# Starting every transferred SBUF buffer at a multiple of 512 bytes in a fused attention and feed-forward kernel

## The chip, the cores and the metric

The kernel runs on one core of a Trainium2 chip. The metric is the device time of one execution in microseconds (us), of which several runs are taken; the median counts.

## The reference

Two stages follow each other. The first is attention with a local window, a few global keys and a bias that falls linearly with distance; the second is a gated feed-forward layer on its output.

```
scores = q k^T / sqrt(64)                       # 4 batches, 8 heads, 768 rows, 64 columns
keep   = (key < 8) or (0 <= row - key < 96)
scores = where(keep, scores - 2^-(head+1) * distance, -1e9)
x      = softmax(scores) v                      # 3072 rows of 512
h      = x w_in                                 # 512 x 2048
out    = (h * sigmoid(1.702 h)) w_out           # 2048 x 512
```

q, k and v are float32. The two weights arrive as float64 and are converted on the chip.

## The kernel before

The 3072 rows are 24 blocks of 128. A block's keys are its own 128 and the last of the block before, with the 8 global keys copied over a few columns of these. The first four blocks (one for each batch) have no block before them, and are computed by another path. Numbers are carried as pairs of float16, a high and a low part, and a product is three matmuls (high times high, high times low, low times high).

For a later block, `prep` (L561) loads q, k and v into `raw` (L443), splits q and k into float16 pairs in `qk` (L510 on ScalarE, L511 on VectorE), turns them by a transposing DMA into `QK` (L513), and makes a second copy of the turned keys with its two halves swapped by two plain DMAs (L515). `halves` (L518) splits v into `VR`. For each pair of heads, `unit` (L574) computes scores on TensorE (L591), adds the mask and takes the minimum on VectorE (L597, into `NM`), exponentiates on ScalarE (L607, the sums of exponentials into `sm`), splits the probabilities `p` into `hl` (L611, L612), turns `hl` by a transposing DMA into `pt` (L613), and multiplies by the values on TensorE (L622 to L624). `finish` (L719) divides by the sums (L739 to L741), splits into `x16` (L763, L765) and turns that into `xT` (L766). `handover` (L546) does the same preparation for the keys and values of a batch's first block: its buffers carry `over` in their names. It also keeps the 8 global keys in `KG` (L527, copied into each block's keys at L538) and the global values in `VG` (L533, copied at L715).

The weights are loaded into `ws` (L238), converted on VectorE and ScalarE (L412 to L418) and kept in SBUF as float16 pairs. The feed-forward layer takes two blocks at a time: `up` (L853) and, for later pairs, `up_two` (L893, with sums at L898 to L909) compute h, L862 to L865 and L925 to L934 the gated product `g`, and `pile` (L961) the sum over 2048 rows of the second weight, written out from `yo` (L977, L994). Late in the run inputs and weights are loaded once more for range checks (`again`).

The order of the instructions is made by a planner (`Work.order`, L136) from estimated costs, due times and a table of offsets (`NUDGE`, L30); every engine then runs its fixed list, and waits by semaphores where data isn't there. SP's queue issues nearly all DMAs, in the planner's order.

A buffer of the planner is a `Buf` in a `Ring` of a few slots (L83 to L105). When a `Buf` is first used, it takes a tile from a pool by its tag, or, where its ring has fixed tiles (`r_hl`), a view of one of these. Two pools lie one behind the other in SBUF: `const`, with what lives through the run, and `sb`, with the rings. A tile's size is rounded up to 32 bytes per partition, and the next begins there, so that one tile of odd size moves the beginnings of all behind it.

Of the kernel before, what the change touches and what calls it, by code (L numbers as in the profile page):

```python
# [8 lines left out]
F32 = mybir.dt.float32  # L9
# [10 lines left out]
P = 128  # L20
# [62 lines left out]
class Ring:  # L83


    def __init__(self, pool, tag, bufs, loose=False, psum=False):
        self.pool, self.tag, self.bufs, self.loose, self.line, self.psum = pool, tag, bufs, loose, [], psum
        self.tiles = None


class Buf:
# [8 lines left out]
    def __call__(self):  # L100
        if self.ring.tiles:
            return self.view(self.ring.tiles[self.i % self.ring.bufs])
        if self.t is None:
            self.t = self.ring.pool.tile(self.shape, self.dtype, tag=self.ring.tag, name=self.name, bufs=self.ring.bufs)
        return self.t  # L105


# [12 lines left out]
class Work:  # L120
# [5 lines left out]
    def add(self, on, fn, after=(), bufs=(), want=1e9):  # L126
        t = Task(on, fn, [a for a in after if a is not None], bufs, want)
        t.tag = self.tag + ("l" if "SP" in on else "")
        for a in t.after:
            a.next.append(t)  # L130
        for b in t.bufs:
            b.users.append(t)
        self.tasks.append(t)
        return t
# [107 lines left out]
def kernel(  # L242
# [12 lines left out]
    B, H, S, D = q.shape  # L255
# [11 lines left out]
    const = ctx.enter_context(tc.tile_pool(name="const", bufs=1))  # L267
# [30 lines left out]
    swt = const.tile([P, 2, NST], F32, name="swt")  # L298
    e2 = const.tile([P, 2, 4 * NST], F32, name="e2")
    junk = const.tile([P, 1024], BF16, name="junk")  # L300
    back = const.tile([P, 1], F32, name="back")
    nc.vector.memset(back, 0.5 / (SG * SW))


    def ring(tag, bufs, pool=sb, loose=False):
        return Ring(pool, tag, bufs, loose, pool is not sb)

    r_raw, r_qk16, r_QK, r_KG = ring("raw", 2), ring("qk16", 1), ring("QK", 3), ring("KG", 1)
    r_VR, r_VG, r_sm = ring("VR", 4), ring("VG", 1), ring("sm", 3)
    r_pr, r_hl, r_pt = ring("pr", 2), ring("hl", 2), ring("pt", 4)  # L310
    r_hl.tiles = [const.tile([P, 8 * P], F16, name=f"hl{j}") for j in range(2)]
    r_VF = ring("VF", 3, loose=True)
    r_x, r_x16, r_xT, r_xS = ring("x", 1), ring("x16", 1), ring("xT", 2), ring("xS", 2)
    r_ws, r_wa = ring("ws", 3), ring("wa", 2, loose=True)
# [80 lines left out]


    WT, W_ready, squared, checks = {}, {}, {}, []

    def weights(s, u):

        nm = f"{s}_{u}"
        ws = Buf(r_ws, [P, 1024, 2], I32, "ws" + nm)
        wa = Buf(r_wa, [P, 1024], F32, "wa" + nm)
        w = WT[s, u] = Buf(r_w[s, u], [P, 2, 1024], F16, "w" + nm)
        ai = lambda: wa().bitcast(I32)
        extra = lambda: w().bitcast(I32).rearrange("p z c -> p (z c)")
        low = lambda: w().bitcast(U16).rearrange("p z (c t) -> p (z c) t", t=2)[:, :, 0]
        t0 = add({"SP": 2.75}, lambda e: load_weights(nc, ws(), w_in, w_out, s, u), bufs=[ws])

        t3 = add({"DVE": 0.61}, lambda e: nc.vector.tensor_scalar(  # L412
            extra(), ws()[:, :, 1], -2 ** 31, -2 ** 30, ALU.bitwise_and, ALU.bitwise_xor), [t0], [ws, w])
        t4 = add({"ACT": 1.21}, lambda e: nc.scalar.mul(low(), ws()[:, :, 0].bitcast(U32), LAST * 2.0 ** -29), [t3], [ws, w])
        t5 = add({"DVE": 1.15}, lambda e: nc.vector.scalar_tensor_tensor(
            ai(), ws()[:, :, 1], 3, extra(), ALU.logical_shift_left, ALU.bitwise_xor), [t3, t4], [ws, w, wa])
        t6 = add({"ACT": 0.96}, lambda e: nc.scalar.mul(w()[:, 0], wa(), SW), [t5], [wa, w])
        t7 = add({"DVE": 1.15}, lambda e: nc.vector.scalar_tensor_tensor(  # L418
            w()[:, 1], wa(), SW, w()[:, 0], ALU.mult, ALU.subtract), [t6], [wa, w])
        W_ready[s, u] = t7  # L420
        early_ = s % 2 and u == 0
        checks.append(add({"ACT": 1.05}, lambda e: nc.scalar.activation(
            junk, w()[:, 0], AF.Square, accum_out=swt[:, u, s:s + 1]), [t7], [w], 140.0 if early_ else 270.0 + 18.0 * (2 * s + u)))
        squared[s, u] = checks[-1]
        if not early_:
            checks[-1].soon = 200.0 + 18.0 * (2 * s + u)
# [8 lines left out]
    blk, prev = {}, {}  # L435

    def place(n):

        return (n, 0) if n < EARLY else ((n - EARLY) // (NB - 1), 1 + (n - EARLY) % (NB - 1))

    def load(n, raw, parts=(0, 1, 2)):
        b, i = place(n)
        return [add({"SP": 1.2 if n < 2 and 2 not in parts else 1.35}, lambda e, z=z: nc.sync.dma_start(  # L443
            raw()[:, z], (q, k, v)[z][b, :, i * P:(i + 1) * P, :].rearrange("h p d -> p h d")), bufs=[raw]) for z in parts]
# [9 lines left out]
    def prep_first(n):  # L454

        raw = Buf(r_raw, [P, 3, H, D], F32, f"raw{n}")
        QZ = Buf(r_w[NST - 1 - n // 2, n % 2], [P, 2, NU, P], F32, f"QZ{n}")
        KF = Buf(r_hl, [P, NU, P], F32, f"KF{n}", lambda t: t.bitcast(F32).rearrange("p (u t) -> p u t", u=NU))
        d = blk[n] = dict(QZ=QZ, KF=KF, sm=Buf(r_sm, [P, 2 * H], F32, f"sm{n}"))

        def clean(e):
            for z in range(2):
                part = slice(D * z, D * z + D)
                if e == "ACT":
                    nc.scalar.mul(QZ()[part, 1 - z], idle[part].rearrange("p (u t) -> p u t", u=NU), 0.0)
                else:
                    nc.gpsimd.memset(QZ()[part, 1 - z], 0.0)

        zero = add({"ACT": 1.2} if n < 2 else {"POOL": 1.2}, clean, bufs=[QZ], want=-10.0 if n < 2 else 1e9)
        ld = load(n, raw, (0, 1))  # L470
        turned = []
        for z in range(2):
            tq = Buf(r_y[1, z] if n == 0 else r_h, [P, NU, P], F32, f"tq{n}_{z}")

            def turn(e, z=z, tq=tq):
                for u in range(NU):
                    nc.tensor.transpose(tq()[:, u], raw()[:, z, 2 * u:2 * u + 2, :].rearrange("p h d -> p (h d)"), ident)

            turned.append((tq, add({"PE": 4 * TURN}, turn, ld[z:z + 1], [raw, tq])))

        def taken(to, z, part):
            tq, t1 = turned[z]
            return add({"ACT": 0.6, "DVE": 0.7}, lambda e: (
                nc.scalar.mul(to(), tq()[part], SX) if e == "ACT" else nc.vector.tensor_scalar(to(), tq()[part], SX, None, ALU.mult)),
                [t1], [tq, KF if z else QZ])

        rows = [slice(D * z, D * z + D) for z in range(2)]
        d["qk_ready"] = [zero, *(taken(lambda z=z: QZ()[rows[z], z], 0, rows[z]) for z in range(2)), taken(KF, 1, slice(0, P))]
# [10 lines left out]
    def turn_halves(n, raw, QK, ld, a0):  # L499

        qk = Buf(r_qk16, [P, 2, H, 2, D], F16, f"qk16{n}_{a0}")

        def rq():
            return raw()[:, a0:2].rearrange("p a h d -> p (a h) d")

        def part(z):
            return qk()[:, a0:, :, z].rearrange("p a h d -> p (a h) d")

        f = 1.0 if a0 == 0 else 0.55
        t1 = add({"ACT": f * 0.96}, lambda e: nc.scalar.mul(part(0), rq(), SX), ld, [raw, qk])  # L510
        t2 = add({"DVE": f * 1.15}, lambda e: nc.vector.scalar_tensor_tensor(part(1), rq(), SX, part(0), ALU.mult, ALU.subtract),  # L511
                 [t1], [raw, qk])
        t3 = add({"SP": f * 2.8}, lambda e: nc.sync.dma_start_transpose(  # L513
            QK()[:, a0:2].rearrange("p a h t -> p (a h) t"), qk()[:, a0:].rearrange("p a h z d -> p (a h z d)")), [t2], [qk, QK])
        return [add({"SP": 0.4}, lambda e, z=z: nc.sync.dma_start(  # L515
            QK()[64 * z:64 * z + 64, 2], QK()[64 - 64 * z:128 - 64 * z, 1]), [t3], [QK]) for z in range(2)]
# [44 lines left out]
    def prep(n):  # L561

        b, i = place(n)
        raw = Buf(r_raw, [P, 3, H, D], F32, f"raw{n}")
        QK = Buf(r_QK, [P, 3, H, P], F16, f"QK{n}")
        d = blk[n] = dict(QK=QK, sm=Buf(r_sm, [P, 2 * H], F32, f"sm{n}"))
        ld = load(n, raw, (0, 1, 2) if n >= EARLY else (0, 1))
        d["qk_ready"] = turn_halves(n, raw, QK, ld[0:2], 0)
        if n >= EARLY:
            VR = d["VR"] = Buf(r_VR, [P, 2, H, D], F16, f"VR{n}")  # L570
            d["v_ready"] = halves(VR, raw, ld[2:])
            guard(n, raw, ld, start[n // 2, 0] - 40.0 + 20.0 * (n % 2))
# [783 lines left out]
```

## Time and profile before

Three runs took 591.45, 592.07 and 594.02 us, a median of 592.07.

| | us |
|---|---|
| profiled execution | 592.54 |
| its span | 590.6 |
| TensorE (PE) busy | 579.0 |
| VectorE (DVE) busy | 497.1 |
| ScalarE (ACT) busy | 462.6 |
| GpSimd (POOL) busy | 3.7 |

In the profile's rows a group of instructions is named by its line, engine, operation and tiles, output first; "<-" names what ended the engine's idle time before it. PEld is the loading of TensorE's weights, which overlaps the matmuls. SPq is SP's queue, where an instruction's length is the time that its issue took. A DMA share of 1 means that the core's 16 DMA engines had packets under way all the time. SP's queue moved 108.30 MB in 268,032 packets, which took 91.2% of the 16 engines' time. The granted clock of TensorE was 1.00 in nearly all stages.

### The profile page before, as it was taken

The page shows a single profiled execution, that of the slowest core. Times are in us where ns is not written, and L with a number is a line of the kernel's source. Part 1 is how long each engine was busy: PE and PEld are TensorE (multiplying, and loading weights), DVE is VectorE, ACT ScalarE, POOL GpSimd, SP SyncE. Part 2 cuts the span into 40 slices and gives each one's busy share as a digit, 9 for nine tenths or more (in the row PEclk, how much of TensorE's full clock was granted, in tenths as well). Part 3 has the DMA queues.
Part 4 walks back from the last instruction along what each step waited for, and adds up shares of the span by engine and source line. Part 5 has one row for each costly group of instructions (what it writes and reads, how often), then busy time and mean ns, then how long its engine had stood idle before and what let it go on. Part 6 is the DMA issues. An engine that isn't in the chain of part 4 may idle for free. (4 is left out here: it accounts for less than half of the span.)

```text
span 590.6 us, 16904 instructions
## 1 busy us (share of the span) xinstructions
PE 579.0 (98%) x6744; PEld 435.4 (74%) x6744; DVE 497.1 (84%) x1180; ACT 462.6 (78%) x1086; POOL 3.7 (1%) x14
## 2 busy tenths in 40 slices
PE   8999899999999999999999999999999999999997
PEld 5886666777678777877778767787777866875896
DVE  6898899999999999888899799889889878676452
ACT  6678799898768979878798798788987878774351
POOL 2000000000000000000000000000000000000000
PEclk9999999999999999999999999999999999999999
DMA  9998999999968877999999999999999999971101
GB/s 256 294 288 204 283 235 239 201 191 164 189 118 170 147 134 145 201 182 202 228 173 203 203 215 206 192 220 205 241 200 169 224 182 228 216 176 19 37 2 41
DMA packets 268265, 109.57 MB, mean 186 GB/s; under 512 B 249300, under 2 KB 249812, under 8 KB 268180
## 3 DMA queue, kind: packets, MB, share of 16 engines
q1 hardware_dynamic: 268032, 108.30, 91.2%
q8 instruction: 54, 0.88, 0.7%
q14 instruction: 31, 0.25, 0.1%
q10 hardware_dynamic: 148, 0.13, 0.1%
HBM read 57.67 MB, written 6.29 MB: 108 GB/s over the span
## 5 line engine op out<-in xcount | busy, mean ns | idle before, releaser
L961 PE MATMUL y<-w,g 128*128 128x512 f16 (+1 forms) x1248 | 265.1, 363 | 1.6 <-DVE g L865 0.8
L961 PEld LDWEIGHTS <-g 128*128 128x128 f16 x1248 | 118.0, 98 | 108.0 <-DVE g L865 1.8
L893 PEld LDWEIGHTS <-w 128*128 128x128 f16 x1728 | 101.4, 98 | 3.9
L607 ACT ACTIVATE p<-p,NM 128x232 f32<-128x232 f32 x160 | 76.4, 479 | 9.4 <-DVE NM L597 9.1
L893 PEld LDWEIGHTS <-T 128*128 128x128 f16 x1296 | 76.8, 98 | 5.7 <-issue 0.4
L853 PE MATMUL h<-xT,w 128*128 128x256 f16 x576 | 67.1, 273 | 0.2 <-DVE t L863 0.2
L597 DVE CUSTOM_DVE_ANT_0 p<-s,mm 128x232 f32<-128x232 f32 x160 | 57.7, 396 | 9.9 <-PE s L591 9.5
L853 PEld LDWEIGHTS <-w 128*128 128x128 f16 x576 | 55.5, 98 | 7.9 <-issue 0.3
L934 DVE SCALAR_TENSOR_TENSOR g<-t,g 128x512 f16<-128x512 f32 x72 | 49.2, 688 | 10.8 <-ACT g L933 10.5
L612 DVE TENSOR_TENSOR hl<-p,hl 128x464 f16<-128x464 f32 x80 | 51.0, 638 | 5.8 <-ACT hl L611 5.6
L933 ACT ACTIVATE g<-t 128x512 f16<-128x512 f32 x72 | 44.9, 628 | 11.7 <-PE y L961 7.8
L925 ACT ACTIVATE t<-h 128x512 f32<-128x512 f32 (+1 forms) x72 | 35.8, 517 | 18.6 <-DVE h L901 15.8
L611 ACT CAST hl<-p 128x464 f16<-128x464 f32 x80 | 46.0, 575 | 1.8 <-DMA pt<-hl 0.3
L893 PE MATMUL pa<-xS,T 128*128 128x128 f16 x648 | 44.8, 219 | 0.0
L901 DVE TENSOR_TENSOR h<-pb,h 128x256 f32<-128x256 f32 x72 | 28.6, 420 | 18.5 <-PE pb L893 17.1
L591 PEld LDWEIGHTS <-QK 128*128 128x128 f16 x640 | 36.5, 98 | 7.1 <-DVE NM L597 1.7
L926 DVE SCALAR_TENSOR_TENSOR t<-t,h 128x512 f32<-128x512 f32 (+1 forms) x72 | 38.5, 553 | 3.3 <-ACT t L925 3.2
L591 PE MATMUL s<-QK 128*128 128x128 f16 x320 | 38.2, 219 | 0.0
L893 PE MATMUL pa<-xT,w 128*128 128x128 f16 x540 | 37.5, 219 | 0.0
L893 PE MATMUL pb<-xS,w 128*128 128x128 f16 x540 | 37.5, 219 | 0.0
L622 PE MATMUL pv<-VR,pt 128*128 128x64 f16 x288 | 34.5, 193 | 0.8 <-DMA VR<-VG 0.5
L624 PE MATMUL pv<-VR,pt 128*128 128x64 f16 x288 | 34.5, 193 | 0.0
(186 smaller groups left out, 1033.7 us busy)
## 6 DMA issues: line engine op xcount, KB each, us to landing
ws<-in_moe_w_in_dram SPq DMA_DIRECT2D x8, 1024.0 KB
ws<-in_moe_w_out_dram SPq DMA_DIRECT2D x8, 1024.0 KB, 6.6
raw<-in_q_dram SPq DMA_DIRECT2D x24, 256.0 KB, 4.5
raw<-in_k_dram SPq DMA_DIRECT2D x24, 256.0 KB, 5.0
QK<-QK SPq DMA_DIRECT2D x40, 128.0 KB, 5.4
raw<-in_v_dram SPq DMA_DIRECT2D x20, 256.0 KB, 3.5
out_dram<-yo SPq DMA_DIRECT2D x20, 256.0 KB
ws_00again<-in_moe_w_in_dram SPq DMA_DIRECT2D x8, 512.0 KB, 4.1
```

What stands on the lines that cost most here:

```text
L591: nc.tensor.matmul(sp()[:, j, lo:hi], d["QK"]()[:, 0, h, :], K[:, 1 + z, h, P - (hi - lo):], start=(z == 0), stop=(z == 1), skip_group_che ...
L597: nc.vector.tensor_tensor_reduce(out=pr()[:, j, :], in0=sp()[:, j, :], in1=m, scale=-1.0 / SC, scalar=3.0e38, op0=ALU.add, op1=ALU.min, ac ...
L607: ex.append(add({"ACT": 0.473}, lambda e, j=j: nc.scalar.activation(pr()[:, j, :], pr()[:, j, :], AF.Exp, bias=NM[:, n, hs[j]:hs[j] + 1], ...
L611: t4 = add({"ACT": 0.5}, lambda e: nc.scalar.copy(hl()[:, 0, :, SKIP:], pr()), ex, [pr, hl])
L612: t5 = add({"DVE": 0.55}, lambda e: nc.vector.tensor_sub(hl()[:, 1, :, SKIP:], pr(), hl()[:, 0, :, SKIP:]), [t4], [pr, hl])
L853: nc.tensor.matmul(ph()[:, fi, :], w1(s, cc, z, fi), X[:, y, cc, :], start=(j + cc == 0), stop=(j == 2 and cc == NCC - 1))
L893: nc.tensor.matmul(o()[:, fi], w, x()[:, y * NCC + 2 * k + cc, t], start=(first and fi + j + cc == 0), stop=(last and j + cc == 3), skip_g ...
L925: t1 = add({"ACT": 0.06 + 0.22 * w}, lambda e: nc.scalar.activation(o(), src(), AF.Tanh, scale=0.851 / (SX * SW)), after, srcs)
L926: return add({"DVE": 0.08 + 0.265 * w}, lambda e: nc.vector.scalar_tensor_tensor(o(), o(), 1.0, src(), ALU.add, ALU.mult), [t1], srcs)
L933: t4 = add({"ACT": 0.53}, lambda e, g=g, tt=tt: nc.scalar.mul(g()[:, 0], tt(), SG / (SX * SW)), u, [tt, g])
L934: t5 = add({"DVE": 0.61}, lambda e, g=g, tt=tt: nc.vector.scalar_tensor_tensor(g()[:, 1], tt(), SG / (SX * SW), g()[:, 0], ALU.mult, ALU.s ...
L961: nc.tensor.matmul(y(), part(zg, f), w2(s, z, f % 2)[:, m], start=(begin and f + j == 0), stop=(end and j == 2 and f == 2 * len(steps) - 1 ...
```

## The change

The change sets where buffers begin in SBUF. The constant `back` becomes a view of a wider tile `room`, a tile `room2` is allocated that nothing uses, the three tiles of `sm` (64 bytes per partition each) go from the pool of rings to the constants, and a tile of `p` is taken with 480 numbers per partition, of which 464 are used as before.

```diff
 class Ring:
-        self.tiles = None
+        self.tiles, self.wide = None, None
 class Buf:
         if self.t is None:
-            self.t = self.ring.pool.tile(self.shape, self.dtype, tag=self.ring.tag, name=self.name, bufs=self.ring.bufs)
+            wide = self.ring.wide
+            self.t = self.ring.pool.tile([P, wide] if wide else self.shape, self.dtype, tag=self.ring.tag, name=self.name,
+                                         bufs=self.ring.bufs)
+            if wide:
+                self.t = self.t[:, 0:self.shape[1] * self.shape[2]].rearrange("p (a w) -> p a w", a=self.shape[1])
...
-    back = const.tile([P, 1], F32, name="back")
+    room = const.tile([P, 16], F32, name="room")
+    back = room[:, 0:1]
...
     r_hl.tiles = [const.tile([P, 8 * P], F16, name=f"hl{j}") for j in range(2)]
+    r_sm.tiles = [const.tile([P, 2 * H], F32, name=f"sm{j}") for j in range(3)]
+    r_pr.wide = 480
...
+    const.tile([P, 16], F32, name="room2")
...
-        d = blk[n] = dict(QZ=QZ, KF=KF, sm=Buf(r_sm, [P, 2 * H], F32, f"sm{n}"))
+        d = blk[n] = dict(QZ=QZ, KF=KF, sm=Buf(r_sm, [P, 2 * H], F32, f"sm{n}", lambda t: t))
...
-        d = blk[n] = dict(QK=QK, sm=Buf(r_sm, [P, 2 * H], F32, f"sm{n}"))
+        d = blk[n] = dict(QK=QK, sm=Buf(r_sm, [P, 2 * H], F32, f"sm{n}", lambda t: t))
```

The built programs have the same instructions on every engine, in the same order and with the same waits on semaphores; only addresses differ. These are the beginnings, in bytes above a multiple of 512 per partition:

| buffers | before | with the change |
|---|---|---|
| `hl` | 480 | 0 |
| `raw`, `ws`, `wa`, `x16`, `pt`, `t` (also holds `yo`) | 224 | 0 |
| the weights of steps 0, 6 and 7 | 224 | 0 |
| `qk`, `QK`, `VR`, `x`, `g`, the first two slots of `xT`, most other weights | 416 | 0 |
| `VG`, the other two slots of `xT` and `xS`, one weight | 288 | 0 |
| `KG` | 416 | 0 |
| `VF` (three slots; also holds `h0` and `h1`) | 128, 160, 192 | 416, 448, 480 |
| `p` (two slots) | 160, 480 | 256, 128 |
| `mm` | 480 | 192 |
| `idle`, `ident`, `id16` | 320 | 320 |
| `mT` (two), `NM` | 64, 320, 64 | the same |

Before, none of the beginnings in the first six rows is a multiple of 64 bytes; in `VF` two of three slots are (128 and 192), and with the change one (448).

## Prediction

> **What bounds the kernel now.** I read the busy times on the page first, then the table by stages, then TensorE's own waits, and last the order of time around the largest of these waits. The first row is the page's first part (busy time and share of the span of each engine); the others are stages (length, busy time and instructions of each engine, granted clock, busy share of the DMA engines, GB/s).
>
> ```profile
> PE 579.0 (98%) x6744; PEld 435.4 (74%) x6744; DVE 497.1 (84%) x1180; ACT 462.6 (78%) x1086; POOL 3.7 (1%) x14
> ...
> 50.00:100.00 50.00, 47.71 (x396) 32.78 (x395) 45.57 (x80) 42.65 (x77) 0.00 (x0) 1.00 1.08 256
> 100.00:150.00 50.00, 49.34 (x493) 36.26 (x491) 48.43 (x108) 45.40 (x103) 0.00 (x0) 1.00 1.01 189
> 150.00:200.00 50.00, 50.00 (x590) 37.57 (x587) 49.03 (x106) 38.72 (x91) 0.00 (x0) 1.00 0.83 158
> ...
> 300.00:350.00 50.00, 50.00 (x670) 38.41 (x668) 43.46 (x123) 42.81 (x116) 0.00 (x0) 1.00 1.04 201
> ```
>
> TensorE is busy for 579.0 of 590.6 us, and from 150 us on it has no gap. The DMA engines are also nearly always busy (shares of 0.83 to 1.08), but that is not the limit: where their share is 1.04, TensorE is busy for 50.00 of 50.00 us at the full granted clock. A transfer is worth time only where TensorE waits for it. These are all of TensorE's waits in the run that the profile lists (total us, times, longest):
>
> ```profile
> PE idle L1139 <- POOL idle L287: 1.3, 1, 1.3
> PE s L591 <- DVE QKover L538: 1.0, 1, 1.0
> PE tq L477 <- ACT QZ L484: 0.8, 1, 0.8
> PE y L961 <- DVE g L865: 0.8, 1, 0.8
> PE s L591 <- DVE NM L597: 0.7, 2, 0.5
> PE y L961 <- ACT g L933: 0.6, 1, 0.6
> PE pv L622 <- DMA VR<-VG: 0.5, 1, 0.5
> PE s L664 <- ACT hl L484: 0.4, 1, 0.4
> PE aux L672 <- DVE top L669: 0.3, 1, 0.3
> PE pv L622 <- DMA pt<-hl: 0.3, 1, 0.3
> PE tx L755 <- DVE x L735: 0.3, 1, 0.3
> PE pb L893 <- DVE t L926: 0.2, 1, 0.2
> PE h L853 <- DVE t L863: 0.2, 1, 0.2
> ```
>
> They sum to 7.4 us, of which only 0.8 us ends on a DMA by name. That is the first bound: if every wait vanished, the kernel would gain 7.4 us. The rest of the idle 11.6 us (590.6 - 579.0) is the tail after the last matmul.
>
> **The change part by part.** No instruction is added, removed or moved: each engine has the same list in the same order with the same semaphore waits, and SP's queue issues the same transfers. Only addresses in SBUF differ. So the sum has three kinds of term: how engines read the moved buffers, how transfers run, and what follows from a transfer that lands earlier or later.
>
> *Engines.* TensorE first. Two kinds of its rows differ in where the moving operand begins: `idle` lies at a multiple of 64 bytes (320 above a multiple of 512), the second weights of L961 at 32 above one (224, 288 or 416 above a multiple of 512).
>
> ```profile
> 6.83 0.81 PE L1139 MATMUL idle<-idle 128*128 128x512 bf16 x3
> 7.48 0.60 PE L477 MATMUL tq<-ident,raw 128*128 128x128 f32 x4
> ...
> 299.67 2.32 PE L961 MATMUL y<-w,g 128*128 128x512 f16 x10
> 301.83 0.83 PE L893 MATMUL pa<-xT,T 128*128 128x128 f16 x12
> ```
>
> From start to next start this is (7.48 - 6.83) / 3 = 0.217 us for the aligned operand and (301.83 - 299.67) / 10 = 0.216 us for the other. Alignment to 64 bytes is worth nothing to a matmul, and I cost it at 0 us. For VectorE the nearest row is L901, whose buffers `h0` and `h1` lie in a ring with two slots at multiples of 64 bytes and one at 32 above (after the change it is two the other way round):
>
> ```profile
> L901 DVE TENSOR_TENSOR h<-pb,h x72: 414/420/426, 186.2 to 573.7; 128x256 f32<-128x256 f32 x72
> ```
>
> The spread of 12 ns between the shortest and the longest of 72 instructions leaves at most 12 ns for it, and each shorter tile stands beside a TensorE that has no gap. ScalarE's moved tiles `sm` hold 64 bytes per row, 16 numbers; I cost them at 0 too. The cover is TensorE's full stage; were it gone, 108 such instructions at 12 ns would be 1.3 us.
>
> *Transfers.* What a start at a multiple of 512 bytes does to a transfer, no row measures directly. The nearest rows are the medians from issue to landing of three transposing transfers, whose source and destination begin at different offsets above a multiple of 512 (`qk` and `QK` 416 and 416, `hl` and `pt` 480 and 224, `x16` and `xT` 224 and 416 or 288):
>
> ```profile
> pt<-hl SPq DMA_TRANSPOSE x80, 4.5
> ...
> QK<-qk SPq DMA_TRANSPOSE x20, 4.4
> xT<-x SPq DMA_TRANSPOSE x20, 4.6
> ```
>
> They differ by 0.2 of 4.5 us, 4%, although QK moves twice the bytes. I take 5% shorter as the value for all transfers, 0% as the lower bound and 20% as the upper, four times what the rows with different offsets show; a loss of as much isn't excluded by them either.
>
> *What waits for them.* Here are the rows of the stage with the largest stalls, and of the one later wait on a DMA (start, length, engine, what; in brackets the idle time before and what ended it):
>
> ```profile
> 50.37 0.37 SPq L238 DMA_DIRECT2D ws<-in_moe_w_out_dram  x1
> ...
> 54.44 6.19 SPq L513 DMA_TRANSPOSE QKover<-qk16over  x1
> ...
> 60.19 0.69 DVE L412 TENSOR_SCALAR w<-ws 128x1024 int32<-128x1024 int32 x1 [2.08 <-DMA ws<-in_moe_w_out_dram]
> ...
> 64.33 1.11 SPq L515 DMA_DIRECT2D QKover<-QKover  x2
> 64.41 2.33 PE L961 MATMUL y<-w,g 128*128 128x512 f16 x10 [0.82 <-DVE g L865]
> ...
> 69.87 0.20 DVE L527 COPY KG<-QKover 128x128 f16<-128x128 f16 x1 [1.43 <-DMA QKover<-QKover]
> 70.35 0.25 PE L591 MATMUL s<-QKover,QK 128*128 128x104 f16 x2 [0.98 <-DVE QKover L538]
> ...
> 75.71 0.27 PE L591 MATMUL s<-QKover,QK 128*128 128x104 f16 x2 [0.49 <-DVE NM L597]
> ...
> 254.75 0.71 SPq L715 DMA_DIRECT2D VR<-VG  x1
> ...
> 257.38 0.19 PE L622 MATMUL pv<-VR,pt 128*128 128x64 f16 x1 [0.49 <-DMA VR<-VG]
> ```
>
> Here the profile says more than the list of waits does. The 0.98 us at 70.35 is put down to VectorE, but VectorE itself had stood still for 1.43 us until two transfers of QKover (L515) landed, and these had been held until the transpose issued at 54.44 had landed. The stall belongs to the DMA: 64.33 - 54.44 = 9.9 us for the transpose, then 69.87 - 64.33 = 5.5 us for the swap of halves, 15.4 us in a row. The 0.82 us at 64.41 also hangs on a DMA: VectorE had waited 2.08 us for weights issued at 50.37.
>
> These stalls must not be added. TensorE's order is fixed, and a stall ends at a time that something else sets: if it reaches 70.35 earlier, it waits longer there. What counts is how much earlier the *last* of a row of stalls ends. At 5% the QKover chain is 0.05 x 15.4 = 0.77 us earlier. The weights would be 0.05 x (60.19 - 50.37) = 0.49 us earlier, which is absorbed at 70.35. The wait at 75.71 is for VectorE, busy without a break since 69.87; it moves with the copy there, by 0.77 us. From there on VectorE is the fullest beside TensorE (48.43 of 50 us from 100 to 150), so the shift holds but doesn't grow; the 0.3 us for `pt` (0.05 x 4.5 = 0.23 us) is in that stage and I count it as absorbed. From 150 us to the next wait TensorE carries the shift through without a gap. At 257.38, VR<-VG took 257.38 - 254.75 = 2.6 us, and 5% of it is 0.13 us. The waits at the start and at 519 (ACT g) are on engines, not transfers: 0.
>
> The sum is 0.77 + 0.13 = 0.9 us less. The profiled execution took 592.54 us, 590.6 of it span and 1.9 around it; it becomes 591.6. That execution lies 0.47 above the median of the three runs, 592.07, so against the median the sum gives 592.07 - 0.9 = **591.2 us**. The bounds: 0% gives 592.1; at 20% the two terms are 3.1 and 0.5, but the first cannot exceed the stalls there that it feeds, 0.82 + 0.98 + 0.49 + 0.3 = 2.6, so 592.07 - 3.1 = 589.0. The same 20% as a loss has no such cap: 592.07 + 3.6 = 595.7.
>
> The Trainium skill speaks for larger gains: by "DMA: Bandwidth & Descriptors", section "How a descriptor splits into AXI transactions", a transaction must start at a multiple of 256 bytes, so that a read that doesn't start there fetches bytes which it throws away. By its count a 2048-byte row that starts 224 bytes above such a multiple costs 71 beats instead of 64, an estimate of 10% less time after the change; a piece of 256 bytes costs 15 instead of 8. It tells this of reads, and in the loads SBUF is written. By 10% on every transfer the sum above would give 1.5 + 0.3 = 1.8 us, 590.3. No row here separates the two.
>
> **The rivals.** (1) *Nothing happens*: transfers are paced by something that addresses in SBUF don't touch, such as the memory they come from or the issue on SP's queue (the transpose at 54.44 alone holds the queue for 6.19 us). For it: the 4% between rows of different offsets may be only noise. Then 592.1. (2) *Transfers are 20% or more shorter*: the stalls named end, 589.0, and where VectorE's work then also lies earlier, the 0.2 us rows go too, 588.6. For it: DMA shares of about 1 in nearly every stage. The skill's rule on 256-byte pieces would be this case. Against it: stalls on VectorE take the place, as it is busy for 48.43 of 50 us. (3) *Slower*: with every buffer on the same offset, transfers that are in flight together meet at the same place in SBUF, and land later. The place is the QKover chain, and the price is 15.4 us x the loss plus 2.6 us x the loss: 1.8 us at 10%, 593.9; it decides (over 0.5%) from 17%, 18.0 x 0.17 = 3.1 us, 595.1. Against it: QK<-qk, whose ends both lie at 416, is the quickest of the three rows, not the slowest. (4) *TensorE reads faster* from aligned buffers: the 0.217 and 0.216 us above speak against it; 1% of 579.0 us would be 586.3.
>
> **How the numbers follow.** Chances: the forecast (590.3 to 591.7) 0.45, nothing happens (591.7 to 592.6) 0.27, transfers much shorter (588.4 to 589.6) 0.17, slower 0.07, TensorE faster 0.04. A measurement of this kernel can tell about 0.5% from no change, 3 us: the three runs spread over 2.6 us. Faster by that means under 589.1: nearly all of the 0.17, and 0.04, less a little, 0.20. Slower means over 595.0, most of the 0.07 and some drift: 0.06. The rest, 0.74, is no change. The range from 588.8 to 593.0 leaves out the slower cases, TensorE's, and the far end of the quick ones, about 0.18.
>
> **What would show it.** Right: the medians of the three transposing rows fall from 4.4 to 4.6 by some tenths of a us; VectorE's 1.43 us before the copy at L527 and TensorE's 0.98 us at L591 shrink; TensorE's busy time stays at 579 within 1 us and the mean of L901 at 420 ns. Wrong: TensorE's starts of L961 come closer than 0.216 us; or the medians of landing fall by 1 us and more and the time doesn't follow beyond 3 us (then VectorE holds it), or they rise. If the time falls below 588 us, my cap on the stalls was too low.

## Result and profile after

Seven runs of the changed kernel took 587.09 to 590.28 us, a median of 588.59; seven of the kernel before, between them, 590.96 to 594.02, a median of 592.07. The ratio is 0.9937 with a 95% interval of 0.9919 to 0.9954: the change is 3.5 us faster, 0.6%. The prediction was 591.2 us in a range from 588.8 to 593.0, so the time lies just below the range, where the second rival was. Medians and ratios leave out two executions, of 1554 and 3142 us, that occurred among the runs of the experiments.

The profiled execution took 587.09 us, 585.2 of it span. It is the quickest of its seven (1.5 us below their median), and the one shown of before lies 0.5 above its own; that is why the two profiles are 5.4 us apart and the medians only 3.5. These are rows of the page of the kernel after, busy times and SP's DMA queue (packets, MB, share of 16 engines):

```profile
PE 577.2 (99%) x6744; PEld 435.0 (74%) x6744; DVE 497.1 (85%) x1180; ACT 461.5 (79%) x1086; POOL 3.7 (1%) x14
...
q1 hardware_dynamic: 268032, 108.30, 83.3%
```

The same row of the page of the kernel before:

```profile
q1 hardware_dynamic: 268032, 108.30, 91.2%
```

The queue moved the same packets and bytes, and they kept the DMA engines busy for 83.3% of the span in place of 91.2%: 0.833 x 585.2 = 487.5 us in place of 0.912 x 590.6 = 538.6, 9.5% less. The DMA issues of the kernel after (KB each where given, median us from issue to landing last; before: 6.6, 4.5, 5.0, 4.5, 4.4 and 4.6 in this order):

```profile
ws<-in_moe_w_out_dram SPq DMA_DIRECT2D x8, 1024.0 KB, 5.7
raw<-in_q_dram SPq DMA_DIRECT2D x24, 256.0 KB, 4.2
raw<-in_k_dram SPq DMA_DIRECT2D x24, 256.0 KB, 5.3
...
pt<-hl SPq DMA_TRANSPOSE x80, 2.9
...
QK<-qk SPq DMA_TRANSPOSE x20, 3.8
xT<-x SPq DMA_TRANSPOSE x20, 4.9
```

The largest fall is in `pt<-hl`, 1.6 us; `xT<-x` and the loads of k land 0.3 us later. A landing is counted from the issue and includes the time in which a transfer stands behind others, so one row doesn't tell what that transfer itself costs. Nor are these medians sharp: `pt<-hl` shows 2.9 here, but 3.5 in the variant below with all buffers at 256, and among the variants with all of them off a multiple of 256 the two slower in time show 3.9 and the two quicker 4.5 and 4.6. All of TensorE's waits in the kernel after:

```profile
PE idle L1147 <- POOL idle L291: 1.3, 1, 1.3
PE tq L485 <- ACT QZ L492: 0.8, 1, 0.8
PE s L599 <- DVE NM L605: 0.5, 2, 0.3
PE aux L680 <- DVE top L677: 0.4, 1, 0.4
PE s L672 <- ACT hl L492: 0.3, 1, 0.3
PE tx L763 <- DVE x L743: 0.3, 1, 0.3
PE h L861 <- DVE t L871: 0.2, 1, 0.2
```

(Lines are numbered 4 to 8 higher than before, and 6 higher again in variants with gaps.) The sum is 3.8 us, before it was 7.4. Gone are the waits on QKover, VR, `pt`, both on `g`, and the one of L893 on `t`. Stages of the kernel after, with the columns of the prediction's first fence:

```profile
50.00:100.00 50.00, 49.65 (x416) 34.57 (x415) 47.52 (x89) 44.53 (x82) 0.00 (x0) 1.00 1.01 273
100.00:150.00 50.00, 49.63 (x501) 36.53 (x499) 48.54 (x105) 45.32 (x102) 0.00 (x0) 1.00 0.88 187
150.00:200.00 50.00, 50.00 (x576) 37.01 (x575) 49.23 (x111) 38.77 (x94) 0.00 (x0) 1.00 0.72 153
...
250.00:300.00 50.00, 50.00 (x630) 36.81 (x628) 42.20 (x106) 41.50 (x104) 0.00 (x0) 1.00 0.96 197
300.00:350.00 50.00, 50.00 (x669) 38.09 (x667) 43.69 (x116) 43.08 (x116) 0.00 (x0) 1.00 0.96 203
...
500.00:550.00 50.00, 49.88 (x587) 36.46 (x585) 34.08 (x85) 31.57 (x79) 0.00 (x0) 1.00 0.51 120
```

Two stages of the kernel before that the prediction doesn't show:

```profile
250.00:300.00 50.00, 49.51 (x622) 36.06 (x620) 41.54 (x102) 39.66 (x100) 0.00 (x0) 1.00 1.07 197
...
500.00:550.00 50.00, 49.05 (x607) 36.11 (x605) 34.05 (x80) 32.54 (x85) 0.00 (x0) 1.00 0.70 137
```

The DMA share fell in every stage, and four of them gave TensorE time: it was busy for 49.65 us in place of 47.71 from 50 to 100, and in the stages from 100, 250 and 500 us on it gained 0.3, 0.5 and 0.8. The order of time around QKover in the kernel after:

```profile
53.61 4.88 SPq L521 DMA_TRANSPOSE QKover<-qk16over  x1
58.31 0.69 DVE L420 TENSOR_SCALAR w<-ws 128x1024 int32<-128x1024 int32 x1 [1.25 <-DMA ws<-in_moe_w_out_dram]
...
62.07 1.11 SPq L523 DMA_DIRECT2D QKover<-QKover  x2
...
66.60 0.20 DVE L535 COPY KG<-QKover 128x128 f16<-128x128 f16 x1
...
67.38 0.26 PE L599 MATMUL s<-QKover,QK 128*128 128x104 f16 x2
...
72.61 0.27 PE L599 MATMUL s<-QKover,QK 128*128 128x104 f16 x2 [0.35 <-DVE NM L605]
```

From the transpose's issue to the swap's it is 62.07 - 53.61 = 8.5 us (9.9 before), and from there to VectorE's copy 4.5 (5.5 before). VectorE comes to the copy with no idle time and TensorE to the scores with no stall.

**Where the 5.4 us of the two profiles lie.** The same matmul starts earlier by 0.8 us at 26 us (26.10 to 25.27), by 3.1 at 75.71 (72.61 above), 3.1 at 118, 4.3 at 375 and 452, and the span ends 5.4 earlier. So 0.8 came in the first 26 us, 2.3 around QKover, 1.2 between 118 and 375, and 1.1 after 452. Of the 1.2, 0.3 lies at the wait on `pt`, 0.65 at the one on VR, and 0.25 at 323 and 327 us, where no wait is listed. The four variants below with every buffer off a multiple of 256 gain 0.3 to 0.7 at VR and 0.2 to 0.25 at 323 and 327 as well, so that these two parts aren't shown to come from alignment. The first 0.8 comes from the pace of TensorE at the start. First the row of before, then of after, ten matmuls of the warm-up on a tile that no DMA touches and that kept its address:

```profile
1.33 4.45 PE L1139 MATMUL idle<-idle 128*128 128x512 bf16 x10 [1.33 <-POOL idle L287]
```

```profile
1.33 3.64 PE L1147 MATMUL idle<-idle 128*128 128x512 bf16 x10 [1.33 <-POOL idle L291]
```

In both, these matmuls start 0.43 us apart at first and 0.22 later. The change of pace comes where the trace lists the granted clock at 1.00 for the first time, 4.0 us after the start in the kernel after and 6.5 in the one before. Of the variants below, which share these instructions, the one with all buffers at 256 has the early clock too (4.0 us, 3.62 for the row); the ten others have it at 5.4 to 7.4 us, the one with `pt` alone off at 6.4, and rows of 4.32 to 4.45. That it differs between executions whatever the addresses is likely, since the two early ones were also the quickest executions of their kernels, 1.5 and 1.6 us below the medians; with one trace of each kernel it is not shown.

Of the 1.1 us at the end 0.1 lies behind TensorE's last matmul, and 1.0 comes from a place that the prediction had put down to engines. The kernel before, in order of time:

```profile
514.73 0.63 ACT L925 ACTIVATE t<-h 128x512 f32<-128x512 f32 x1 [2.15 <-DMA out_dram<-yo]
...
519.62 3.06 PE L961 MATMUL y<-w,g 128*128 128x512 f16 x12 [0.64 <-ACT g L933]
```

The kernel after:

```profile
509.37 0.63 ACT L933 ACTIVATE t<-h 128x512 f32<-128x512 f32 x1 [1.10 <-DMA out_dram<-yo]
...
514.27 3.06 PE L969 MATMUL y<-w,g 128*128 128x512 f16 x12
```

TensorE waits for ScalarE's `g` at 519.62, but ScalarE itself had stood for 2.15 us until an output transfer let go of a slot that `yo` shares with `t`, and from 514.73 on it was busy without a break until it had written that `g`. In the kernel after the same instruction waits 1.10 us. Three matmuls of TensorE that had come 0.35, 0.80 and 0.28 us late against the pace around them, at 517.12, 519.62 and 520.35, now come 0, 0.12 and 0.28 late. Measured by the starts of the same matmuls around 514 to 525 us, the four variants with every buffer off are 0.3 to 0.6 us slower than before, and the seven others 0.8 to 1.5 quicker. Around QKover the four gain 0.3 to 1.0 us, the seven 0.9 to 2.1.

### The profile page after: what moved, and what is told of

The parts are those of the page before. It is cut to its first block, busy times and chain, and to the rows that moved or that the text cites. A ratio compares the mean times of both kernels' runs of the same rounds, so it can differ in the third digit from the quotient of the medians.

```text
span 585.2 us, 16904 instructions
## 1 busy us (share of the span) xinstructions
PE 577.2 (99%) x6744; PEld 435.0 (74%) x6744; DVE 497.1 (85%) x1180; ACT 461.5 (79%) x1086; POOL 3.7 (1%) x14
## 3 DMA queue, kind: packets, MB, share of 16 engines
q1 hardware_dynamic: 268032, 108.30, 83.3%
## 5 line engine op out<-in xcount | busy, mean ns | idle before, releaser
L901 PEld LDWEIGHTS <-w 128*128 128x128 f16 x1728 | 101.4, 98 | 3.9
L901 PEld LDWEIGHTS <-T 128*128 128x128 f16 x1296 | 76.8, 98 | 5.2 <-issue 0.2
L942 DVE SCALAR_TENSOR_TENSOR g<-t,g 128x512 f16<-128x512 f32 x72 | 49.0, 685 | 11.8 <-ACT g L941 11.6
L901 PE MATMUL pa<-xS,T 128*128 128x128 f16 x648 | 44.8, 219 | 0.0
L901 PE MATMUL pa<-xT,w 128*128 128x128 f16 x540 | 37.5, 219 | 0.0
L901 PE MATMUL pb<-xS,w 128*128 128x128 f16 x540 | 37.5, 219 | 0.0
```

The costliest lines, as they stand in the source:

```text
L901: nc.tensor.matmul(o()[:, fi], w, x()[:, y * NCC + 2 * k + cc, t], start=(first and fi + j + cc == 0), stop=(last and j + cc == 3), skip_g ...
L942: t5 = add({"DVE": 0.61}, lambda e, g=g, tt=tt: nc.vector.scalar_tensor_tensor(g()[:, 1], tt(), SG / (SX * SW), g()[:, 0], ALU.mult, ALU.s ...
```

## Experiments

What was to be told apart: whether the gain comes from addresses at all or from the other edits that came with them (the place of `sm`, the width of `p`); where the threshold lies (64, 256 or 512 bytes); whether an odd start costs by its size; and which transfers carry the time.

**All transferred buffers moved together.** Everything behind `room` is pushed up, and the rest of the change stays: by 8 numbers (32 bytes), and in the other kernels by 16, 32, 56 and 64 numbers (64, 128, 224 and 256 bytes).

```diff
-    room = const.tile([P, 16], F32, name="room")
+    room = const.tile([P, 16 + 8], F32, name="room")
```

At 32 bytes:

> The changed kernel with every transferred buffer moved 32 bytes further, so that all begin 32 bytes above a multiple of 512; same instructions, same order. Theory A (what counts is a start at a multiple of 64 bytes): as slow as before, 591 to 593 us, turning of the probabilities (pt<-hl) back at about 4.5 us to landing, share of the DMA engines about 91%. Theory B (what counts is how many bytes of the first 256-byte piece are thrown away, few here): almost as quick as the change, 588 to 589.5 us, pt<-hl near 3 us, share near 84%. Theory C (only a multiple of 512 helps): as before. Theory D (not where transfers begin, but where the small tiles sm lie or that p is wider): 588 to 589.5 us. By the Trainium skill, page DMA: Bandwidth & Descriptors, section How a descriptor splits into AXI transactions, a 2048-byte row here costs 65 beats against 64, which is theory B.

At 64:

> The same with 64 bytes: all transferred buffers begin 64 bytes above a multiple of 512. Theory A: as quick as the change, 588 to 589.5 us, pt<-hl about 2.9 us, share about 83%. Theory B: nearly the same as the change, slightly above 32 bytes' cost: 588.5 to 590 us. Theory C: as before, 591 to 593 us. Theory D: 588 to 589.5 us.

At 128:

> The changed kernel with every transferred buffer 128 bytes above a multiple of 512. After 32, 64 and 224 bytes were about as slow as before and 256 as quick as the change, theory E (what counts is a start at a multiple of 256 bytes; any other start costs the same one more piece, however many bytes of it are used) expects it as before: 591 to 593.5 us, share of the DMA engines 90 to 91%. Theory F (the cost falls step by step with the offset's largest power of two, 64 already a little quicker) expects it between: 589.5 to 591 us, share 86 to 88%.

At 224:

> The same with 224 bytes, the offset that most buffers had before. Theories A, B and C: as before, 591 to 593 us, pt<-hl about 4.5 us, share about 91%. Theory D: 588 to 589.5 us, though pt<-hl lands late again; only this run and 32 bytes tell D from the rest.

At 256:

> The same with 256 bytes. Theories A, B and D: as quick as the change, 588 to 589.5 us, pt<-hl about 2.9 us. Theory C: as before, 591 to 593 us.

| start above a multiple of 512 | median us | ratio to before (95%) | DMA share | QKover stall on TensorE, us |
|---|---|---|---|---|
| 0 (the change) | 588.59 | 0.9937 (0.9919 to 0.9954) | 83.3% | none |
| 256 | 588.69 | 0.9918 (0.9899 to 0.9936) | 83.8% | none |
| 128 | 590.81 | 0.9961 (0.9940 to 0.9982) | 89.6% | 1.4 |
| 64 | 592.36 | 0.9983 (0.9966 to 1.0000) | 90.0% | 0.8 |
| 224 | 593.42 | 1.0004 (0.9981 to 1.0027) | 91.0% | 0.9 |
| 32 | 594.07 | 1.0007 (0.9989 to 1.0025) | 90.4% | 1.1 |

Each ratio is to runs of the kernel before that were taken beside it, so that ratios can be compared between rows more closely than medians. The kernel at 32, its page's queue row:

```profile
q1 hardware_dynamic: 268032, 108.30, 90.4%
```

and at 256:

```profile
q1 hardware_dynamic: 268032, 108.30, 83.8%
```

Pushed off by 32 or 224 bytes, the kernel is as slow as before, with `sm` among the constants and `p` wide: those edits are worth nothing by themselves. 256 is as good as 0, so that 512 isn't needed; 64 and 128 keep the high share and the QKover stall, so that 64 isn't enough. By share the threshold is 256 bytes. By time the kernels at 64 and 128 lie between (0.9983 and 0.9961), the second clearly below 1, and the share doesn't explain that. In the profiles they differ by TensorE's waits for `pt`; first at 32, then at 224, then at 128:

```profile
PE pv L630 <- DMA pt<-hl: 3.8, 5, 1.2
```

```profile
PE pv L630 <- DMA pt<-hl: 1.4, 2, 1.2
```

```profile
PE pv L630 <- DMA pt<-hl: 0.2, 1, 0.2
```

At 64 it is 0.3. These are one execution each, at 32 the slowest of its twelve, and why `pt` comes late there stays open.

**The disputed cost by itself.** A kernel that only transfers: eight loads of 256 KB (pieces of 256 bytes, as `raw`), four of 1 MB (as `ws`), four turning transfers from a buffer at the offset (as `hl` to `pt`), four into one, and eight stores, for each of six offsets, and then for the offsets in the opposite order. VectorE touches each group when it has landed.

```diff
+OFFSETS = (0, 32, 64, 128, 224, 256)
...
+                    if kind == "from":
+                        for j in range(4):
+                            nc.sync.dma_start_transpose(halves(still[:, j * 512:(j + 1) * 512]).rearrange("p (a t) -> p a t", a=8),
+                                                        halves(at(kind, o, j, 512)))
+                        nc.vector.tensor_copy(mark[:, 0:4], still.rearrange("p (j c) -> p j c", j=4)[:, :, 0])
```

> No attention and no layers: only transfers, in groups that each wait for the group before, at the offsets 0, 32, 64, 128, 224 and 256 above a multiple of 512, then once more in reverse order. load: 8 loads of 256 KB into SBUF in pieces of 256 bytes, as of q. weigh: 4 of 1 MB in rows of 2 and 4 KB, as of the weights. from: 4 turning transfers with the source at the offset. to: 4 with the destination there. store: 8 of 256 KB out of SBUF. The output is not the reference's. Theory R (only reading SBUF from such a start costs more, as the Trainium skill, page DMA: Bandwidth & Descriptors, section How a descriptor splits into AXI transactions, tells it): from and store 10% or more longer at 32, 64, 128 and 224 than at 0 and 256, the other three equal within 3%. Theory W (only writing): the other way round. Theory RW (both): all five longer. By theory E the four odd offsets cost the same; by theory F, which the run at 128 bytes spoke for, 128 costs least of the four.

VectorE in order of time in this kernel; the idle time in brackets is that of one group of transfers. First loads at 32, 224 and 256, then turning from 32, 224 and 256, then turning into 32, 224 and 256:

```profile
36.81 0.17 DVE L65 COPY mark<-load 128x8 f32<-128x8 f32 x1 [11.65 <-DMA load<-in_k_dram]
...
71.96 0.17 DVE L65 COPY mark<-load 128x8 f32<-128x8 f32 x1 [11.58 <-DMA load<-in_k_dram]
83.04 0.17 DVE L65 COPY mark<-load 128x8 f32<-128x8 f32 x1 [10.90 <-DMA load<-in_k_dram]
...
175.62 0.17 DVE L76 COPY mark<-still 128x4 f32<-128x4 f32 x1 [7.39 <-DMA still<-from]
...
198.55 0.17 DVE L76 COPY mark<-still 128x4 f32<-128x4 f32 x1 [7.61 <-DMA still<-from]
205.65 0.17 DVE L76 COPY mark<-still 128x4 f32<-128x4 f32 x1 [6.93 <-DMA still<-from]
...
218.18 0.17 DVE L81 COPY mark<-to 128x4 f32<-128x4 f32 x1 [6.93 <-DMA to<-still]
...
239.50 0.17 DVE L81 COPY mark<-to 128x4 f32<-128x4 f32 x1 [6.94 <-DMA to<-still]
246.62 0.17 DVE L81 COPY mark<-to 128x4 f32<-128x4 f32 x1 [6.95 <-DMA to<-still]
```

| group, us in both orders | 32 | 64 | 128 | 224 | multiple of 256 |
|---|---|---|---|---|---|
| load, 256-byte pieces | 11.65, 11.58 | 11.57, 11.60 | 11.48, 11.51 | 11.58, 11.74 | 10.90 (at 256), 11.13 (at 0) |
| turning, source at the offset | 7.39, 7.41 | 7.41, 7.50 | 7.40, 7.49 | 7.61, 7.49 | 6.93 (at 256), 6.94 (at 0) |
| turning, destination at the offset | 6.93, 6.96 | 6.94, 7.21 | 6.93, 6.94 | 6.94, 6.94 | 6.95 (at 256), 6.93 (at 0) |

A start off a multiple of 256 costs a load some 5% (11.59 on average against 11.0) and a turning transfer 8% on the side it reads (7.46 against 6.93), and nothing on the side it writes. The aligned groups in the table are all the last of their kind, and the next kind begins beside them. That place doesn't make a group shorter: among the destinations the last ones, 6.95 and 6.93, are like the others, and the last groups of 1 MB loads are longer (14.55 and 14.27). An odd start costs the same at 32, 64, 128 and 224. The 1 MB loads (13.4 to 13.7 us) and the stores (7.0) are alike at the four odd offsets too, but their aligned groups stood first and last of their kind and overlapped with others, so that what alignment is worth to them was not measured alone. None of the three theories written down for this kernel holds as it stood: reading costs a turning transfer less than 10%, loads that write SBUF cost more too, and 128 is no cheaper than the other odd starts.

**Which buffers carry the time.** A gap puts one part 32 bytes off (`loadsoff`: `raw`, `ws`, `t` with `yo`, and `x16`, 32 bytes below a multiple of 512), and the rest is aligned. It is called "loads" for short, but holds the output's `yo` and one source of turning transfers, `x16`, too.

```diff
+GAPS = {'pt': 8}
...
 class Buf:
...
+            gap = GAPS.pop(self.ring.tag, None)
+            if gap:
+                self.ring.pool.tile([P, gap], F32, tag=f"gap_{self.ring.tag}", name=f"gap_{self.ring.tag}", bufs=1)
...
-    const.tile([P, 16], F32, name="room2")
+    const.tile([P, 8], F32, name="room2")
```

> The changed kernel with the buffers raw, ws, t (also yo) and x16 32 bytes below a multiple of 512, and all others of the transferred ones at a multiple of it. These take in what comes from memory outside, and send out yo and x16. Theory G (the gain comes from the turning transfers hl to pt and qk to QK, and the swap of halves): 588.3 to 589.7 us, share of the DMA engines 83 to 85%, pt<-hl near 3 us. Theory H (it comes from the loads, which fill the DMA engines in the first 60 us): 591 to 593 us, with the stall before the first scores on QKover back at about 1 us.

The opposite, with the buffers of the turning transfers (`hl`, `pt`, `qk`, `QK`, `VR`, `xT`) and `wa` (which the weights are loaded into once more for the range checks) at 32 and the loads aligned, keeps the gap and adds

```diff
-    room = const.tile([P, 16], F32, name="room")
+    room = const.tile([P, 16 + 8], F32, name="room")
```

> The other half: raw, ws, t and x16 begin at a multiple of 512, all other transferred buffers (hl, pt, qk, QK, VR, xT, wa) 32 bytes above one. Theory G: as before, 591 to 593.5 us, share 88 to 91%, pt<-hl 4 to 4.5 us. Theory H: 588.3 to 589.7 us.

With the loads off: 591.04 us, ratio 0.9969 (0.9948 to 0.9990), share 88.2%. With the turned buffers off: 589.76, 0.9937 (0.9915 to 0.9960), share 85.9%. The shares nearly add up (83.3 + 4.9 + 2.6 = 90.8, before 91.2), the times don't: aligned loads alone bring as much as the whole change, aligned turns alone about half. The two intervals overlap a little, so the order is likely and not proven. The QKover place shows a mechanism that fits. With the loads off, in order of time:

```profile
63.85 1.11 SPq L529 DMA_DIRECT2D QKover<-QKover  x2
...
69.27 0.20 DVE L541 COPY KG<-QKover 128x128 f16<-128x128 f16 x1 [1.20 <-DMA QKover<-QKover]
```

With the turned buffers off:

```profile
62.96 1.11 SPq L529 DMA_DIRECT2D QKover<-QKover  x2
...
67.42 0.20 DVE L541 COPY KG<-QKover 128x128 f16<-128x128 f16 x1
```

The swap that TensorE waits for reads and writes QKover. Where QKover is aligned and the loads are not, it takes 69.27 - 63.85 = 5.4 us, as before; where QKover is off and the loads aligned, 4.5 at most, and the stall is gone. The loads of q, k and the weights share the DMA engines with it, and these are full there (1.09 and 1.03 from 50 to 100 us). So it isn't the swap's own addresses that decide here; less work beside it fits, with one execution of each kernel. In the two kernels below with `raw` or `ws` alone off the swap takes 4.8 us.

**Single rings.** `hl` alone at 32 (with `sm` and `mm`, which lie behind it):

```diff
-    room = const.tile([P, 16], F32, name="room")
+    room = const.tile([P, 16 + 8], F32, name="room")
...
-    const.tile([P, 16], F32, name="room2")
+    const.tile([P, 8], F32, name="room2")
```

> The changed kernel with hl alone 32 bytes above a multiple of 512: the source of the 80 transfers that turn probabilities; its small neighbours sm and mm move along. If it is reading that costs more from such a start: pt<-hl at 4 us and more, share 86 to 89%, 589.5 to 592 us. If it is writing: nothing moves, pt<-hl 2.9 to 3.5 us, 588 to 589.5 us. If a part of each counts: between.

588.68 us, 0.9925 (0.9901 to 0.9949), share 85.5%, `pt<-hl` 3.9 us. `pt` alone, by gaps of 8 numbers ahead of it and 56 behind, in the same lines of `Buf` as above:

```diff
+GAPS = {'pt': 8, 'wa': 56}
```

> The changed kernel with pt alone 32 bytes above a multiple of 512: the destination of the 80 transfers that turn probabilities (with hl, their source, so moved, they landed after 3.9 us in place of 2.9, and the time was as quick as the change's). If writing counts as reading does: pt<-hl 3.7 us or more, share 85 to 86%, 588.3 to 589.7 us. If writing of turned blocks is indifferent: pt<-hl 2.9 to 3.5 us, share 83 to 84%, the same time.

588.25 us, 0.9932 (0.9910 to 0.9953), share 84.0%, `pt<-hl` 3.1. The source counts for the share (+2.2), the destination hardly (+0.7); in the landing the source's 3.9 stands against 2.9 to 3.5 in kernels where both ends are aligned. Neither is seen in the time, so that the expected 589.5 us or more for a costly source was missed. In the same manner `raw` alone:

```diff
+GAPS = {'raw': 8, 'w7_1': 56}
```

> The changed kernel with the rings of raw (q, k, v, over and again) alone 32 bytes above a multiple of 512, all other transferred buffers at multiples of 256. If the 256-byte pieces of q, k and v carry the part that the loads have: 590.5 to 592 us, DMA share 87 to 88%, the stall on QKover back at 0.7 us or more. If the weights' rows do: 588.3 to 589.7 us, share 84 to 85%.

589.90 us, 0.9951 (0.9930 to 0.9972), share 87.3%, with the copy at 68.62 behind 0.85 us of waiting and TensorE's QKover stall back at 0.3, less of both than was expected for `raw` (590.5 us or more, 0.7). And `ws` alone:

```diff
+GAPS = {'ws': 8, 'w6_1': 56}
```

> The changed kernel with ws alone 32 bytes above a multiple of 512. If the 256-byte pieces of raw carry the loads' part: 588.3 to 589.7 us, share 84 to 85%, no stall on QKover. If the weights' rows do: 590.5 to 592 us, and that stall back at 0.7 us or more.

589.09 us, 0.9940 (0.9919 to 0.9961), share 82.9%, no QKover stall. This profile is of the slowest of its eight executions (593.77 us, 591.9 of it span), in which TensorE waits 2.0 us for `pt` at 475 to 477 and then has a granted clock of 0.50 for 3.4 us; 82.9% of its span is 490.7 us, 3.2 more than in the kernel after. So `raw` holds most of the loads' share (+4.0 of 4.9), in 88 loads with pieces of 256 bytes, and `ws`, with few and large loads, little. In time the four lie within 1.7 us and their intervals overlap; only `raw` brought the stall back.

## Why the prediction was wrong

**Right:** that engines would gain nothing. Buffers that moved relative to a multiple of 64 changed nothing on TensorE, whose pace stayed 0.216 us for 512 columns; the group of L901 went from 420 to 418 ns. Right too that the stall at 70.35 belongs to the DMA and not to VectorE, that stalls don't add up, and the cap for that stage: 2.6 us at most, 2.3 measured. The second rival, transfers so much shorter that the named stalls end, came nearest (589.0 by its sum, 588.6 measured), at a chance of 0.17. Its condition, 20% on every transfer, was not met, though: single transfers are 5 and 8% longer when off, and the queue's busy time fell by 9.5%. That its sum is so near is in part luck, as it holds nothing for the wait at 519.

**The term that was mis-sized: "5% shorter, as the value for all transfers".** It came from three rows whose ends lay at 416, 480, 224 and 288, and which differed by 4%. None of these is a multiple of 256, and every odd start costs the same, as the kernel of transfers showed: the rows compared bad with bad, and their likeness was no evidence of a small effect. Measured, the queue's busy time fell by 9.5%, and the QKover chain went from 15.4 to at most 13.0 us, 16%. The percentage alone doesn't explain the miss: with 10% the prediction's own sum gives 590.3. Lengthening by queueing was nowhere in it: 5% was put on each transfer by itself, in stages whose DMA share was 1. The swap speaks for such queueing: it took 5.4 us beside misaligned loads and at most 4.5 beside aligned ones. TensorE gained 2.3 us at this place, where the sum had 0.77.

**The step that failed: "The waits at the start and at 519 (ACT g) are on engines, not transfers: 0".** At the start no run contradicts it (the 0.8 us there are the clock's). At 519 it failed: one step further back ScalarE had waited 2.15 us for an output transfer, and TensorE gained 1.0 us there. The prediction had walked back behind VectorE's waits at 64 and 70 and not behind this one.

**Smaller misses.** The wait on `pt`, "counted as absorbed", gave 0.3 us, and the one on VR, at 0.13 us, 0.65, though the second also where buffers are misaligned. That TensorE "has no gap" from 150 us on was misread: it is busy for 49.51 us of the stage from 250 and 49.05 of the one from 500, and two waits of the prediction's own list lie there. TensorE's busy time fell by 1.8 us, not within 1. About 0.8 of that is the warm-up. Most of the rest lies in the stalls that went: at 64.41, 70.35, 128.94, 257.38 and 517.12 each brought the next matmul forward by 0.16 us more than its idle time on record (0.66 for 0.50 at 257.38). The row of `xT<-x` rose by 0.3 us where a fall was forecast. Without the 0.8 of the warm-up the two profiles differ by 4.6 us and the medians by 3.5; single runs spread over 3 us.

Of the rivals, "nothing happens" fell with the share of 83.3%. "Slower" fell with the time, and nothing landed later at QKover. "TensorE faster" fell with the unchanged pace.

The granularity of 256 bytes that the kernels at 224 and 256 show is the one which the Trainium skill states ("DMA: Bandwidth & Descriptors", "How a descriptor splits into AXI transactions"). The estimate of 10% that the prediction worked out from its count is near the 9.5% less busy queue, but this nearness is luck: by the same count a read of 256 bytes from 224 above would take 15 beats in place of 8, and a start at 32 would be nearly free for a row of 2 KB, where turning transfers from 32 and from 224 took 7.39 and 7.61 us and aligned ones 6.93. The section tells this of reads, while here loads that write SBUF cost 5% more as well (11.65 and 11.58 us at 32 and 224, 10.90 at 256).

## What to carry to other kernels

Begin SBUF buffers at a multiple of 256 bytes per partition, those first that are loaded in 256-byte pieces and those that turning transfers read; for destinations of turning transfers, 1 MB loads and stores no gain was shown here. One constant of odd size ahead of the buffers moves them all, and it cost this kernel 0.6% although TensorE was busy for 98% of its time. Before a wait on an engine is costed at nothing, follow that engine's own idle time back until the chain ends at an engine that was busy or at a transfer. And rows tell the price of a property only if they differ in it: ask of each row on which side of the suspected threshold it lies.

## What was not expected of the hardware

- The cost of an odd start doesn't depend on how odd: 32, 64, 128 and 224 bytes above a multiple of 256 gave 7.4 to 7.6 us for four turning transfers that read there, against 6.93.
- It falls on the side that a turning transfer reads, not on the side it writes (6.93 to 6.96 us at all offsets but for one 7.21); but for plain loads it falls on the SBUF side that is written (11.6 against 11.0).
- The swap of QKover, a plain transfer, took 5.4 us beside misaligned loads though its own buffer was aligned, and at most 4.5 us beside aligned loads though its own buffer was not.
- TensorE's matmuls of 512 columns start 0.43 us apart until the granted clock is listed at 1.00, and 0.22 after it; in 13 profiles this came between 4.0 and 7.4 us after the start, which alone is worth 0.8 us between two of them.
- Open: why `pt` comes late in the kernels at 32 and 224, which are a little slower than those at 64 and 128 (1.0007 and 1.0004 against 0.9983 and 0.9961); why the queue's busy time fell by more (9.5%) than either kind of transfer alone (5 and 8%); and what alignment alone is worth to stores and to 1 MB loads.
